# Tile 1's load behind tile 0's, three short warm matmuls, and one matmul moved earlier, in the head of a fused attention and MLP kernel

## Chip, cores, metric

One core of a Trainium2 chip. The metric is the device time of one execution in microseconds; most executions of one kernel lie within 0.3% of each other, which here is 0.4 us. "The span" is the time from the first to the last instruction of the profiled execution; it is 1.4 to 1.7 us shorter than the device time.

## The reference

Layer norm of x (2048 tokens of 448), then two branches on the normalised tokens: linear attention with 16 heads, and an MLP with a squared ReLU; the output is x plus the product of the first and the silu of the second.

```python
xn = layernorm(x)                                   # 2048 x 448, bf16
q, k, v = split(xn @ wqkv)
pq, pk = phi(q), phi(k)                             # phi(t) = t+1 if t>0 else exp(t), + 1e-6
s = ((pq @ (pk.T @ v)) / (pq @ sum(pk) + 1e-6)) @ wo    # per head
h = relu(xn @ w1 + b1) ** 2                         # 2048 x 1792
g = silu(h @ w2 + b2)
return x + s * g
```

## The kernel before

The kernel is a list of operations, put in order per engine by a planner in Python and emitted with semaphores. TensorE and the SP load queue keep the order of the program; VectorE and ScalarE are ordered by the planner's modelled times, except in the head (the first 8 us), where lists pin them.

Tokens are worked on in tiles of 128. The head normalises tiles 0 to 3, turns them with TensorE transposes (`turn`), and feeds the first products: k0 and k1 (keys of tiles 0 and 1) and h0 to h3 (the first four MLP rows). Each product has chunks of 128 of the 448 inputs. The last 64 inputs run on half of the array (64 rows). The first such matmuls, `rests(k0, k1)`, end the head: I call their start **the half-array start**.

```python
# loads, in the order of issue (SP's queue, ACT's queue)
load_x(0, 1)                                   # SP: tile 0
load_x(1, 2, "act").prio = -118                # ACT: tile 1
twins = load_k("sp", w_qkv, A_wqkv, "wk", 384, 2 * D, later=True)   # SP: 384 KB of key weights
load_x(2, 4)                                   # SP: tiles 2 and 3
dma("act", b1r[0:NF, :], ...)                  # ACT: a bias
load_w1("w1a", 0, 512, 2, [twins])             # SP: MLP weights, first part
load_x(4, 8)                                   # SP: tiles 4 to 7
load_w1("w1b", 512, 1024)
# ... (cut)
# the head's order on TensorE
warm(8, wide=True)                             # eight 512-column matmuls on ones: they wake the clock
turn("xT00", 0, (0,), "dve")                   # tile 0, chunk 0; evicted by VectorE
turn("xT01", 0, (1,), "act")
turn("xT02", 0, (2,), "act")
mains(k0, (0,), ...)
turn("xT10", 1, (0,), "act")
mains(k0, (1,), ...)
turn("xT12", 1, (1, 2), "act")
mains(k0, (2,), ...)
mains(k1, (0,), ...)
h_mains(0, (0,))                               # h0, chunk 0: 256 columns
mains(k1, (1, 2), ...)
# bias transpose (cut)
h_mains(0, (1, 2))
turn("xT03", 0, (3,), "act", 2)
h_mains(1)                                     # h1, chunks 0 to 2
turn("xT2", 2, K3, "act")
h_mains(2)
turn("xT3", 3, K3, "dve")                      # tile 3
h_mains(3)
turn("xT23", 2, (3,), "act", 2)
rests(k0, k1)                                  # the half-array start
# pinned orders: st = statistics, mv = mean/variance, ln/ex = logarithm and exponential
# for 1/sqrt, xn = normalise, xd = last 64 columns
("dve", "st0 mv0 st1 mv1 xn00 xn01 xT00 xn10 xn11 st2 mv2 st3 mv3 xn2 xd2 xn3 xd3 xT3"),
("act", "ln0 ex0 ln1 ex1 xT01 xT02 xT10 xT12 ln2 ex2 ln3 ex3 b1 xT03 xT2 xT23"),
```

Of the kernel before, what the change touches and what calls it, by code (L numbers as in the profile page):

```python
# [56 lines left out]
class Program:  # L57
# [8 lines left out]
    def add(self, eng, emit, reads=(), writes=(), dur=0.2, alts=(), nbytes=0):  # L66
        op = Op(eng, emit, reads, writes, dur, alts, nbytes)
        for t in op.reads:
            w = self.writer.get(t)
            if w is not None:  # L70
                op.raw.add(w)
            self.readers.setdefault(t, []).append(op)
        for t in op.writes:
            w = self.writer.get(t)
            if w is not None and w is not op:
                op.deps.add(w)
            for r in self.readers.get(t, ()):
                if r is not op:
                    op.deps.add(r)
            self.writer[t] = op  # L80
            self.readers[t] = [r for r in self.readers.get(t, ()) if r is op]
        op.raw.discard(op)
        op.deps |= op.raw
        for d in op.deps:
            d.succ.append(op)
        self.ops.append(op)
        return op
# [203 lines left out]
def bass_recurrent_scan__linear_attn_block__dense_activation_squared_relu__prompt_kernel(  # L291
# [4 lines left out]
    with ExitStack() as es:  # L296
# [11 lines left out]
        ones = sb("ones", [P, 2], bf)  # L308
# [95 lines left out]
        def dma(eng, dst, src, writes, nbytes, reads=()):  # L404
            return add(eng, lambda e, _: e.dma_start(dst, src), reads, writes, 0.5, nbytes=nbytes)

        def load_x(lo, hi, eng="sp", reads=()):
            names = [("x", i) for i in range(lo, hi)]
            return dma(eng, x_tok[:, lo:hi, :], x_r[:, lo:hi, :], names, (hi - lo) * P * D * 2, reads)

        def load_k(eng, w, src, name, lo, hi, eng2=None, reads=(), later=False):

            n = (hi - lo) * 2
            dma(
                eng, w[:, 0:3, lo:hi], src[0:384, lo:hi].rearrange("(c p) j -> p c j", p=P), [(name, 0)], 384 * n,
                reads,
            )
            def twins():
                for i in (0, 1):
                    dma(eng2 or eng, w[64 * i : 64 * i + 64, 3, lo:hi], src[384:448, lo:hi], [(name, 1 + i)], 64 * n)  # L420

            if later:
                return twins
            twins()
# [18 lines left out]
        table = add("act", lambda e, _: e.preload_act_table_set("natural_log_exp_and_others"), [], ["actw"], 0.1)  # L443
        table.prio = -120
        load_x(0, 1)
        load_x(1, 2, "act").prio = -118
        twins = load_k("sp", w_qkv, A_wqkv, "wk", 384, 2 * D, later=True)
        load_x(2, 4)
        dma("act", b1r[0:NF, :], B_b1.rearrange("(f p) -> f p", p=P), ["b1r"], F * 2, ["b1r"]).prio = -115
# [73 lines left out]
        def turn(name, si, chunks, eng, tiles=1):  # L523


            b = Buf("T")
            pieces = [(si + t, c) for t in range(tiles) for c in chunks]
            n = len(pieces)
            for i, (t, c) in enumerate(pieces):
                reads = xn_of(t)[min(c, 1) :][:1] or xn_of(t) if c < 3 else [("xd", t)]  # L530
                add(
                    "pe",
                    lambda e, _, i=i, t=t, c=c: e.transpose(  # L533
                        ps(b)[:, i * 64 : (i + 1) * 64].bitcast(bf), xn[:, t, c * P : (c + 1) * P], ident[:, :]
                    ),
                    reads + ["ident"] + ([b] if i else []), [b], 0.06,
                )

            def ev(e, _):
                src = ps(b)[:, 0 : n * 64].bitcast(bf)  # L540
                dst = xT[:, chunks[0], si * P : (si + tiles) * P]
                if len(chunks) > 1:
                    src = src.rearrange("p (c k) -> p c k", c=n)
                    dst = xT[:, chunks[0] : chunks[0] + n, si * P : (si + 1) * P]
                if eng == "dve":
                    return e.tensor_copy(dst, src)
                return e.activation(out=dst, in_=src, func=AF.Copy)  # L547

            dur = 0.06 + 0.09 * n if eng == "dve" else 0.16 + 0.11 * n
            head[name] = add(eng, ev, [b], [("xT", t, c) for t, c in pieces], dur)  # L550
# [51 lines left out]
        def mains(u, ks=K3, reads=None):  # L602


            def f(e, _):
                for k in ks:
                    last = u.mm(e, 2, k, k == 0, False)
                return last

            reads = u.reads if reads is None else reads  # L610
            add("pe", f, reads + ([u.bank] if ks[0] else []), [u.bank], len(ks) * MM(u.n))
# [10 lines left out]
        def phi(buf, slot, tile, shape):  # L622

            src = lambda: shape(ps(buf)[:, 0:512])
            add("act", lambda e, _: e.activation(out=slot, in_=src(), func=AF.Exp), [buf, "actw"], [tile], 0.6)  # L625
            add(
                "dve",
                lambda e, _: e.tensor_scalar(
                    out=slot, in0=slot, scalar1=1.0, scalar2=1e-6, op0=ALU.min, op1=ALU.add
                ),  # L630
                [tile], [tile], 0.25,
            )
            add(
                "dve",
                lambda e, _: e.scalar_tensor_tensor(  # L635
                    out=slot, in0=src(), scalar=1.0 + 1e-6, in1=slot, op0=ALU.add, op1=ALU.max
                ),
                [tile, buf], [tile], 0.69,
            )

        def kk(si):


            b = Buf("K")

            def mm(e, h, c, start, stop):
                return e.matmul(  # L647
                    ps(b)[:, 0:512], xT[half[h], c, si * P : (si + 1) * P], w_qkv[half[h], c, 384 : 2 * D],
                    start=start, stop=stop,
                )  # L650

            return Acc(b, xT_of(si) + wnames("wk"), mm, lambda: phi(b, qk_of(si), ("pk", si), blocks), 512)
# [419 lines left out]
        def warm(n, wide=False, after=()):  # L1072
            b = Buf("W")
            w = 512 if wide else P

            def f(e, _):
                for _i in range(n):
                    last = e.matmul(ps(b)[:, 0:w], junk[:, 0:P], junk[:, 0:w], start=True, stop=True)
                return last

            add("pe", f, ["ones", *after], [b], n * (0.426 if wide else 0.107))

        warm(8, wide=True)
        k0, k1 = kk(0), kk(1)
        first = [hh(0, fi, 0) for fi in range(4)]
        second = [hh(0, fi, 1, first[fi].bank) for fi in range(4)]

        def h_mains(fi, ks=K3):
            xs = xT_of(0) + xT_of(1)
            mains(first[fi], ks, [x for x in xs if x[2] in ks] + [("w1a", fi // 2 * 3)])  # L1090
# [2 lines left out]
        turn("xT00", 0, (0,), "dve")  # L1093
        turn("xT01", 0, (1,), "act")
        turn("xT02", 0, (2,), "act")
        mains(k0, (0,), [("xT", 0, 0)] + wk0)
        turn("xT10", 1, (0,), "act")
        mains(k0, (1,), [("xT", 0, 1)])
# [1 line left out]
        mains(k0, (2,), [("xT", 0, 2)])  # L1100
        mains(k1, (0,), [("xT", 1, 0)] + wk0)
        h_mains(0, (0,))
        mains(k1, (1, 2), [("xT", 1, 1)])
        bb = Buf("B1")
        b1v = lambda: ps(bb)[:, 0 : P // 2].bitcast(bf)
# [3 lines left out]
        )  # L1109
        h_mains(0, (1, 2))  # L1110
        turn("xT03", 0, (3,), "act", 2)
        h_mains(1)
        turn("xT2", 2, K3, "act")
        h_mains(2)
        turn("xT3", 3, K3, "dve")
# [158 lines left out]
```

## Time and profile before

| | before |
|---|---|
| device time, median of 3 | 141.1 us (140.84 to 141.34) |
| span of the profiled run | 139.4 us |
| TensorE busy | 98% |
| first transpose / half-array start | 4.17 / 8.57 us |

The profile has PE for TensorE's matmuls, PEld for its weight loads, DVE for VectorE, ACT for ScalarE. A timeline line reads: start, length, engine, source line, operation, output<-inputs, shapes, count, and in brackets the idle time just before and what ended it. A matmul's length includes its drain, so how long it occupies TensorE is read from the distance to the next start. The prediction below shows the lines of the kernel before.

### The profile page before, as it was taken

What the parts mean: (1) busy time and instruction counts of PE and PEld (TensorE: products, weight loads), DVE (VectorE), ACT (ScalarE), POOL (GpSimd) and SP (SyncE); (2) the same over time, 40 slices, a digit from 0 to 9 for tenths busy, and PEclk for the clock granted to TensorE, in tenths of its full rate; (3) what the DMA queues carried; (4) which work ended last, traced back from release to release, by engine and by line L of the source; (5) the groups of instructions that cost most, each with busy time, mean ns of one, the idle gap of its engine ahead of it and who ended that gap; (6) DMA issues with size and microseconds to landing.
All of it is one profiled execution on the core that took longest, in us unless ns stands there. A gap on an engine that the chain in (4) does not pass through costs nothing.

```text
span 139.4 us, 3131 instructions
## 1 busy us (share of the span) xinstructions
PE 136.4 (98%) x1271; PEld 69.3 (50%) x1271; DVE 92.9 (67%) x227; ACT 78.2 (56%) x153; POOL 22.9 (16%) x35
## 2 busy tenths in 40 slices
PE   9999999999999999999999999999999999999993
PEld 2484444444444444444555455645555555555472
DVE  3989798898888997789896920218936072452743
ACT  4679789788988887979887922512033030300221
POOL 2810000000000000000910000000001419092680
DMA  6996557999822300000000046970000102112132
GB/s 194 249 340 207 90 159 172 362 281 145 139 52 55 67 9 5 0 19 5 0 0 0 28 120 168 182 113 3 0 0 5 66 0 98 39 59 73 35 102 66
DMA packets 20353, 12.90 MB, mean 93 GB/s; under 512 B 9524, under 2 KB 19956, under 8 KB 20340
## 3 DMA queue, kind: packets, MB, share of 16 engines
q1 hardware_dynamic: 18332, 11.52, 33.1%
q10 hardware_dynamic: 2008, 1.19, 4.3%
q8 instruction: 10, 0.16, 0.5%
q14 instruction: 3, 0.02, 0.1%
HBM read 8.78 MB, written 2.10 MB: 78 GB/s over the span
## 4 chain that ended last, share of the span: by engine, by line
PE 95%; DMA 2%; DVE 2%; ACT 0%; issue 0%
PE pb L969 31%; PE pb L694 30%; PE pb L647 9%; PE pb L1037 8%; PE pb L728 7%; PE pb L678 6%; DMA x_tok<-in_A_x_dram 2%; PE pb L735 1%; PE pb L533 1%; DVE st L467 1%; PE pb L829 1%; PE pb L790 1%; PE pb L867 0%; DVE mv L468 0%; DVE xn L1005 0%; ACT gbuf L945 0%
## 5 line engine op out<-in xcount | busy, mean ns | idle before, releaser
L694 PE MATMUL pb<-xT,w 64*128 64x512 bf16 (+2 forms) x408 | 51.9, 365 | 0.0
L969 PE MATMUL pb<-w,r 64*128 64x448 bf16 (+3 forms) x406 | 44.9, 343 | 0.0
L703 ACT ACTIVATE r<-pb,b1f 128x512 bf16<-128x512 f32 x56 | 35.1, 688 | 3.3 <-PE pb L694 3.3
L694 PEld LDWEIGHTS pb<-xT,w 64*128 64x128 bf16 (+1 forms) x408 | 23.3, 94 | 21.0 <-DVE qk L635 0.3
L969 PEld LDWEIGHTS pb<-w,r 64*128 64x128 bf16 (+1 forms) x406 | 22.8, 95 | 20.0 <-issue 0.7
L945 ACT ACTIVATE gbuf<-gbuf 128x448 bf16<-128x448 bf16 (+1 forms) x16 | 8.7, 567 | 36.3 <-DVE gbuf L980 35.6
L980 DVE TENSOR_TENSOR gbuf<-pb,b2b 128x448 bf16<-128x448 f32 (+1 forms) x16 | 9.3, 610 | 28.3 <-PE pb L969 28.3
L1016 POOL TENSOR_TENSOR xn<-xn,x_tok 128x448 bf16<-128x448 bf16 x15 | 15.1, 1031 | 50.7 <-DVE xn L1005 50.7
L647 PE MATMUL pb<-w_qkv,xT 64*128 64x512 bf16 (+1 forms) x106 | 18.1, 378 | 0.0
L678 PE MATMUL pb<-xT,w_qkv 64*128 64x512 bf16 x84 | 15.6, 376 | 0.0
L711 DVE TENSOR_TENSOR r<-r 128x512 bf16<-128x512 bf16 x42 | 14.6, 416 | 0.9 <-ACT r L703 0.9
L394 POOL MEMSET kvm<- 128x2048 bf16 x1 | 1.8, 1804 | 58.5 <-DVE zb L672 58.5
L467 DVE BATCH_NORM_STATS2 st<-x_tok 128x6 f32<-128x448 bf16 x16 | 9.3, 612 | 2.6 <-DMA x_tok<-in_A_x_dram 2.6
L1037 PE MATMUL pb<-msb,pqT 64*128 64x448 bf16 (+3 forms) x93 | 10.9, 343 | 0.0
L635 DVE SCALAR_TENSOR_TENSOR qk<-pb,qk 128x512 bf16<-128x512 f32 x16 | 10.6, 684 | 0.2
L625 ACT ACTIVATE qk<-pb 128x512 bf16<-128x512 f32 x16 | 8.9, 595 | 3.0 <-PE pb L647 2.5
L1005 DVE TENSOR_TENSOR xn<-pb,gbuf 128x448 bf16<-128x448 f32 (+2 forms) x17 | 9.2, 591 | 1.8 <-ACT gbuf L945 1.1
L647 PEld LDWEIGHTS pb<-w_qkv,xT 64*128 64x128 bf16 (+1 forms) x106 | 6.8, 94 | 6.2 <-ACT xT L547 0.5
L728 PE MATMUL pb<-qk,xn 128*128 128x448 bf16 x48 | 9.3, 353 | 0.0
L678 PEld LDWEIGHTS pb<-xT,w_qkv 64*128 64x128 bf16 x84 | 6.1, 94 | 4.8
L712 ACT ACTIVATE r<-r 128x512 bf16<-128x512 bf16 x14 | 8.4, 638 | 0.0
L666 DVE TENSOR_TENSOR zacc<-zacc,qk 128x448 f32<-128x448 f32 x13 | 8.1, 623 | 0.3
(74 smaller groups left out, 97.3 us busy)
## 6 DMA issues: line engine op xcount, KB each, us to landing
out_dram<-xn SPq DMA_DIRECT2D x15, 112.0 KB, 1.7
w<-in_B_w_dram SPq DMA_DIRECT2D x1, 1568.0 KB, 10.0
x_tok<-in_A_x_dram SPq DMA_DIRECT2D x3, 448.0 KB, 3.8
xT<-rows ACTq DMA_DIRECT2D x6, 112.0 KB
w<-in_B_w_dram SPq DMA_DIRECT2D x1, 576.0 KB, 5.7
xT<-rows SPq DMA_DIRECT2D x5, 112.0 KB
w_o<-in_A_wo_dram SPq DMA_DIRECT2D x1, 392.0 KB, 11.1
w_qkv<-in_A_wqkv_dram SPq DMA_DIRECT2D x1, 384.0 KB, 3.7
```

The source lines that it names most:

```text
L467: add("dve", lambda e, _: e.bn_stats(st6[:, si, :], x_tok[:, si, :]), [("x", si)], [("st", si)], 0.58),
L635: lambda e, _: e.scalar_tensor_tensor(out=slot, in0=src(), scalar=1.0 + 1e-6, in1=slot, op0=ALU.add, op1=ALU.max),
L647: return e.matmul(ps(b)[:, 0:512], xT[half[h], c, si * P : (si + 1) * P], w_qkv[half[h], c, 384 : 2 * D], start=start, stop=stop,)
L678: return e.matmul(ps(b)[:, 0:512], w_qkv[half[h], c, m * P : (m + 1) * P], xT[half[h], c, g * 512 : (g + 1) * 512], start=start, stop=stop,)
L694: return e.matmul(ps(b)[:, c0 : c0 + n], w_1[half[h], c, fi * P : (fi + 1) * P], xT[half[h], c, t : t + n], start=start, stop=stop,)
L703: lambda e, _: e.activation(out=slot, in_=ps(b)[:, 0:512], func=AF.Relu, bias=b1f[:, fi : fi + 1]),
L711: return e.tensor_tensor(out=slot, in0=slot, in1=slot, op=ALU.mult)
L728: last = e.matmul(ps(b)[:, 0:D], xn[:, si, c * P : (c + 1) * P], pk_of(si), start=(si == 0), stop=(si == NT - 1),)
L969: return e.matmul(ps(b)[:, 0:n], r2[half[h], fi, si * P : (si + 1) * P], w_2[half[h], fi, c], start=start, stop=stop)
L980: "dve", lambda e, _: e.tensor_tensor(out=gs, in0=ps(b)[:, 0:n], in1=b2b[:, c], op=ALU.add),
L1016: eng, lambda e, _: e.tensor_tensor(out=ob, in0=ob, in1=x_tok[:, si, c], op=ALU.add),
L1037: return e.matmul(ps(b)[:, 0:n], q, m, start=start, stop=stop)
```

## The change

The intent, as read from the edit: tile 0's load should not share the DMA engines with tile 1's; the clock should not fall asleep in the hole between the warm matmuls and the first transposes; and a hole of 0.1 us before k1's second chunk should be filled.

```diff
-        load_x(1, 2, "act").prio = -118
+        load_x(1, 2, "act", ["ones"]).prio = -118
...
         warm(8, wide=True)
+        warm(2)
...
         turn("xT02", 0, (2,), "act")
+        warm(1)
         mains(k0, (0,), [("xT", 0, 0)] + wk0)
...
         h_mains(0, (0,))
+        h_mains(1, (0,))
         mains(k1, (1, 2), [("xT", 1, 1)])
...
         turn("xT03", 0, (3,), "act", 2)
-        h_mains(1)
+        h_mains(1, (1, 2))
         turn("xT2", 2, K3, "act")
```

## The prediction

> **What bounds the kernel now.** I read the page first. The TensorE (PE) row is busy for 136.4 of 139.4 us and the chain that ended last is PE for 95%, so time can be won only where PE stands idle or runs slowly. The change touches only the first 8 us, so I then read the timeline of PE there, the chain in order of time, and the timelines of VectorE (DVE), ScalarE (ACT) and the DMA queues around each hole.
>
> ```profile
> span 139.4 us, 3131 instructions
> PE 136.4 (98%) x1271; PEld 69.3 (50%) x1271; DVE 92.9 (67%) x227; ACT 78.2 (56%) x153; POOL 22.9 (16%) x35
> PE 95%; DMA 2%; DVE 2%; ACT 0%; issue 0%
> ...
> 0.30 3.60 PE L1078 MATMUL pb<-ones 128*128 128x512 bf16 x8 [0.30 <-DVE ones L358]
> 4.17 0.71 PE L533 MATMUL pb<-ident,xn 128*128 128x128 bf16 x3 [0.27 <-DVE xn L490]
> 4.77 0.58 PE L647 MATMUL pb<-w_qkv,xT 128*128 128x512 bf16 x1
> 5.17 0.24 PE L533 MATMUL pb<-ident,xn 128*128 128x128 bf16 x1
> 5.25 0.38 PE L647 MATMUL pb<-w_qkv,xT 128*128 128x512 bf16 x1
> 5.46 0.28 PE L533 MATMUL pb<-ident,xn 128*128 128x128 bf16 x2
> 5.57 0.59 PE L647 MATMUL pb<-w_qkv,xT 128*128 128x512 bf16 x2
> 6.00 0.27 PE L694 MATMUL pb<-xT,w 128*128 128x256 bf16 x1
> 6.21 0.60 PE L647 MATMUL pb<-w_qkv,xT 128*128 128x512 bf16 x2
> ```
>
> A matmul's duration includes its drain; the time it takes from the next one is the distance between starts. The eight warm matmuls lie 0.427 us apart (3.60 less one drained 0.63, over 7 is 0.424), so the last one starts at 3.27 and stops feeding at 3.70. Then: idle to 4.17; three transposes held to the pace of DVE (starts 4.17, 4.48, 4.56); the first matmul of k0 at 4.77, which takes 0.40 before the next start, where those at 5.57 take 0.22 each; and a hole between h0's first chunk (6.00, 0.11 us of feeding) and 6.21. From there I found starts back to back until 8.42, a change of row mode of 0.10 at 8.57, then nothing open until 74 us.
>
> What sets 4.17 is the chain from tile 0's load: landing, then four DVE instructions in order (tile 1's statistics stand before tile 0's normalisation):
>
> ```profile
> 0.00 2.32 DMA x_tok<-in_A_x_dram
> 2.34 0.63 DVE L467 BATCH_NORM_STATS2 st<-x_tok 128x6 f32<-128x448 bf16 x1 [2.14 <-DMA x_tok<-in_A_x_dram]
> 3.00 0.18 DVE L468 BATCH_NORM_AGGREGATE mv<-st 128x2 f32<-128x6 f32 x1
> 3.10 0.59 DVE L467 BATCH_NORM_STATS2 st<-x_tok 128x6 f32<-128x448 bf16 x1
> 3.73 0.18 DVE L468 BATCH_NORM_AGGREGATE mv<-st 128x2 f32<-128x6 f32 x1
> 3.83 0.60 DVE L490 TENSOR_SCALAR xn<-x_tok,mv,rstd 128x128 bf16<-128x128 bf16 x2
> ```
>
> The last thing to read is what the head feeds into. PE's only early wait after it is a weight load at 11.36:
>
> ```profile
> 8.89 1.15 DVE L467 BATCH_NORM_STATS2 st<-x_tok 128x6 f32<-128x448 bf16 x2 [0.30 <-DMA x_tok<-in_A_x_dram]
> 10.43 0.30 ACT L477 ACTIVATE vep<-mv,eps 128x2 f32<-128x2 f32 x1 [0.34 <-DVE mv L468]
> 10.63 0.67 ACT L703 ACTIVATE r<-pb,b1f 128x512 bf16<-128x512 f32 x1
> 10.54 1.03 PE L647 MATMUL pb<-w_qkv,xT 64*128 64x512 bf16 x8
> 11.36 0.36 PEld L694 LDWEIGHTS pb<-xT,w 64*128 64x128 bf16 x6 [0.29 <-DVE qk L635]
> 11.40 0.60 PE L694 MATMUL pb<-xT,w 64*128 64x512 bf16 x4
> ```
>
> The load is put down to DVE, but DVE's first eviction (10.48 plus 0.68) was done at 11.16, 0.2 before; ACT's eviction of h0 ends at 10.63 + 0.67 = 11.30, and 0.06 is what such a release takes elsewhere (DVE ends 4.11, PE starts 4.17). So I take ACT as the releaser. ACT came late because it stood 0.34 for the statistics of tiles 4 and 5, and those stood 0.30 for their load, issued at 4.96 and landing 3.9 later on a busy DMA (shares of 9 in most slices from 5 to 9). Nothing in that chain depends on PE's head. PE arrives at 11.40 with 0.04 us to spare.
>
> **What the Trainium skill says.** "TensorE: Matmul & The Clock Gate", Part 1, has PE start at half clock and go to full after a busy window of about 3.4 us that runs free of the kernel; 512 columns then take 426.7 ns cold and 215.7 warm. The trace agrees: 0.427 before, 0.22 from 5.25 on. The 0.40 at 4.77 is nearly all cold, so in this execution the step came at about 5.15 (0.375 cold and 0.026 warm make up 512 columns). The profile's granted clock reads 1.000 throughout and does not show this step. Part 4 of the same page says transposes do not count as busy in the same way; no view here shows it. "DMA: Bandwidth & Descriptors", Issuing engines are not separate DMA queues, says loads issued from SP and ACT run on the same 16 engines and interleave: the trace has tile 1's packets (second queue) beside tile 0's from 1.3 us on.
>
> **The change part by part.**
>
> Tile 1's load. ACT now issues it at 0.15; it will wait for the ones, set at 0.14 + 0.06 = 0.20. PE waits for the same and starts at 0.30, so the issue moves by about 0.15 to 0.30. It takes 2.4 us to land: 2.70 in place of 2.55 (more exactly 2.59). DVE wants it at 3.10, so 0.4 is left: no loss. The gain is what tile 0 stops losing to it. The DMA view in slices of 0.1 us gives 16 packets for the first queue at 1.2 with the second silent, and 17 at 1.6 beside 15 of the second: tile 0 is not slowed while its 128 packets go out (1.0 to 1.8). Only the last 0.5 us to landing can shorten. I take 0.05, at most the 0.15 of the shift.
>
> Two warm matmuls behind the eight: 2 x 0.107 (a quarter of 0.427 each) in the hole from 3.70 to 4.17: end 3.91, off the path. Cost 0.
>
> One warm matmul before k0: the third transpose starts at 4.56 and feeds 0.107 cold, to 4.67; k0 starts at 4.77, released by the DVE copy (4.49 + 0.22 = 4.71). The hole is 0.10, the matmul 0.107: cost 0.01.
>
> h1's first chunk behind h0's: 256 columns, 0.107 to 0.11 us, same weight piece and same inputs as h0's chunk at 6.00, so no new wait. It fills the hole from 6.11 to 6.21, which ends by ACT's eviction (5.45 + 0.71 = 6.16). It is taken from its place after 7.04, so PE saves 0.11 there less 0.01 of delay: 0.10.
>
> Clock. If the step stays at 5.15, work moved 0.05 earlier runs at half speed: -0.02. In the executions where added activity brings it forward to before 4.77, k0's first matmul gives 0.19 more.
>
> Sum at 8.57: 0.05 - 0.01 + 0.10 - 0.02 = 0.12 us earlier. But at 11.36 PE meets the ACT chain, which is tied to the load of tiles 4 to 7. Only the 0.04 of slack gets through; the other 0.08 turns into idle before 11.40. With 0.04 off 141.1 it is 141.06.
>
> **The rivals.**
>
> The planner reorders. The kernel orders ACT and DVE by modelled times, and these move a little with the warm matmuls and h1. If ACT evicts h0 before the logarithm of tiles 4 and 5, the gate falls and all 0.12 arrives: about 141.0. For: h0's product is nearly complete when ACT stands idle for 0.34. Against: the first orders are pinned, and the modelled load does not move. I give it 35%.
>
> The warm matmuls work through the clock. Then the head gains 0.2 to 0.3 more, and the time is 140.8 where the gate is open. For: the hole from 3.70 to 4.17 lies in the window. Against: even without them the window up to 5.15 was enough to raise the clock, and 0.32 us of work is under a tenth of 3.4. 15%.
>
> The gate lies elsewhere in most executions: the three runs span 0.5 us, so the clock's phase and DMA times differ. Where the head is later than in the profile (141.34), the change gains its full 0.12 or more.
>
> Loss: tile 1 late, a bad eviction order or a clock step that fails. The 0.4 of slack and the unchanged order of loads speak against it; it would make 141.3 to 141.6. 10%.
>
> **Range and chances.** Weighted: half at 0.04, a third at 0.12, the rest between 0.3 and -0.3, gives about 0.1 to 0.15. I say 140.95. The runs of one kernel spread by 0.25 to either side, and a median of three halves that, plus the 0.3 a moved clock or order is worth: 140.5 to 141.3. For 2% it would need 2.8 us; all holes of the head together (0.47, 0.20, 0.10, 0.18 cold, 0.10) make about 1.05. So within 2%: 0.98.
>
> **What would show it right or wrong.** Right: ACT's queue issues tile 1 at about 0.30, it lands near 2.7; tile 0's first statistics start within 2.20 to 2.34; two chunks of 256 columns stand between 5.9 and 6.2 with no hole; the row-mode change comes 0.1 to 0.15 earlier than 8.57; and the 512-column H matmuls still start at about 11.35 behind a PE hole of near 0.1. Wrong: PE passes 11.4 with no hole and early (planner), the first k0 matmul taking 0.22 (clock), or statistics of tile 1 waiting for a DMA.

## The result, and the profile after

The changed kernel takes 141.00 us (median of 6, 140.84 to 141.27) against 140.97 for the one before (6 runs). The ratio is 1.0002, 95% interval 0.9984 to 1.002: the same. The interval is wider than the gain that was predicted, so the times alone can neither show nor exclude a gain of 0.1 us. A ratio here is the mean time of one kernel's fast runs over that of the other's of the same rounds, so not quite the ratio of the medians quoted.

From the page of the changed kernel:

```profile
span 139.3 us, 3137 instructions
PE 136.3 (98%) x1274; PEld 68.5 (49%) x1274; DVE 93.0 (67%) x227; ACT 78.2 (56%) x153; POOL 22.9 (16%) x35
```

From its timeline of PE:

```profile
0.30 3.52 PE L1078 MATMUL pb<-ones 128*128 128x512 bf16 x10 [0.30 <-DVE ones L358]
...
4.10 0.60 PE L533 MATMUL pb<-ident,xn 128*128 128x128 bf16 x3 [0.28 <-DVE xn L490]
4.53 0.22 PE L1078 MATMUL pb<-ones 128*128 128x128 bf16 x1
4.65 0.39 PE L647 MATMUL pb<-w_qkv,xT 128*128 128x512 bf16 x1
...
5.97 0.39 PE L694 MATMUL pb<-xT,w 128*128 128x256 bf16 x2
6.20 0.59 PE L647 MATMUL pb<-w_qkv,xT 128*128 128x512 bf16 x2
...
7.79 0.34 PE L533 MATMUL pb<-ident,xn 128*128 128x128 bf16 x3
...
8.51 0.39 PE L647 MATMUL pb<-w_qkv,xT 64*128 64x512 bf16 x2
```

Compare line by line. The first transpose starts at 4.10 in place of 4.17. k0's first matmul starts at 4.65 in place of 4.77 and already runs at full clock: in this execution the clock stepped up at 3.39, during the eighth wide warm matmul, before any of the added ones ran. So PE had gained 0.23 us by k1's first chunk (5.56 in place of 5.79, the second start of the x2 lines). Then most of it is gone: h0's and h1's chunks start at 5.97 (h0's was at 6.00), k1's second at 6.20 (6.21), now with h1's chunk already done. At the first chunk of h2 PE is 0.14 ahead (7.40 in place of 7.54), about what the prediction had summed up; it then stands idle 0.06 before tile 3's transposes. At 8.51 the head is 0.06 ahead, and it stays so to the end: the last matmul starts at 136.74 in place of 136.81.

Two waits took the gain. The first is in the view of waits of PE's weight loads between 5 and 9 us; the second shows on DVE's timeline, where tile 3's normalisation ends at 7.32 + 0.41 = 7.73, and the transposes of it start 0.06 later (above, 7.79):

```profile
PEld pb L694 <- DMA w<-in_B_w_dram: 0.4, 1, 0.4
...
5.15 0.63 DVE L467 BATCH_NORM_STATS2 st<-x_tok 128x6 f32<-128x448 bf16 x1
...
7.32 0.41 DVE L490 TENSOR_SCALAR xn<-x_tok,mv,rstd 128x384 bf16<-128x384 bf16 x1
```

The kernel before has the same wait in reach; its lines of DVE and PE are

```profile
7.33 0.41 DVE L490 TENSOR_SCALAR xn<-x_tok,mv,rstd 128x384 bf16<-128x384 bf16 x1
...
7.87 0.33 PE L533 MATMUL pb<-ident,xn 128*128 128x128 bf16 x3
```

There TensorE came to tile 3 last, without idling; but VectorE had it ready only 0.07 earlier (7.33 + 0.41 + 0.06 = 7.80).

The first wait is not one of h1's chunk. It is that of h0's chunk for the first MLP weights, which landed at 5.92; the kernel with the short warm matmuls alone, without h1's chunk, has it too (landed 6.06, start 6.10).

The statistics of tile 2 at 5.15 follow the landing of tiles 2 and 3, which the trace puts at 5.13. In the kernel before these statistics started at 5.17, after VectorE's own work. From tile 2's statistics to tile 3's transposes it is a fixed chain (2.61 to 2.64 us in the seven executions where TensorE waits for it).

The gate that the prediction named is there, but open. PEld's line of it:

```profile
11.22 0.22 PEld L694 LDWEIGHTS pb<-xT,w 64*128 64x128 bf16 x4 [0.21 <-DVE qk L635]
```

The weight load came at 11.22 for a matmul at 11.34, and PE did not idle there. In this execution tiles 4 to 7 landed at 8.72 and not at 8.87, and ScalarE's eviction ended at 11.15 in place of 11.30.

### The profile page after: what moved, and what is told of

It is laid out like the page before. It is cut to its first block, busy times and chain, and to the rows that moved or that the text cites. A ratio compares the mean times of both kernels' runs of the same rounds, so it can differ in the third digit from the quotient of the medians.

```text
span 139.3 us, 3137 instructions
## 1 busy us (share of the span) xinstructions
PE 136.3 (98%) x1274; PEld 68.5 (49%) x1274; DVE 93.0 (67%) x227; ACT 78.2 (56%) x153; POOL 22.9 (16%) x35
## 4 chain that ended last, share of the span: by engine, by line
PE 95%; DVE 2%; DMA 2%; ACT 0%; issue 0%
PE pb L969 31%; PE pb L694 31%; PE pb L647 9%; PE pb L1037 8%; PE pb L728 7%; PE pb L678 7%; DMA x_tok<-in_A_x_dram 2%; PE pb L735 1%; DVE st L467 1%; PE pb L829 1%; PE pb L533 1%; PE pb L790 1%; PE pb L867 0%; DVE xn L490 0%; DVE mv L468 0%; DVE xn L1005 0%
## 5 line engine op out<-in xcount | busy, mean ns | idle before, releaser
L694 PEld LDWEIGHTS pb<-xT,w 64*128 64x128 bf16 (+1 forms) x408 | 22.7, 94 | 22.1 <-DMA w<-in_B_w_dram 0.4
```

The costliest lines, as they stand in the source:

```text
L694: return e.matmul(ps(b)[:, c0 : c0 + n], w_1[half[h], c, fi * P : (fi + 1) * P], xT[half[h], c, t : t + n], start=start, stop=stop,)
```

## The experiments

Twelve kernels, each with a profile, so twelve more executions to read. The theories, as they were formed: **A**, VectorE paces the head; **B**, TensorE paces it and the parts add as in the prediction; **C**, three things decide together (the clock's step, VectorE's chain, the load of tiles 4 to 7); **D**, the form of C with numbers that the first ten traces gave. All results were correct.

### The load alone (e1_load)

Edit: only `load_x(1, 2, "act", ["ones"])`.

> Only tile 1's load behind the ones. Theory A (up to 7.8 us the head is paced by VectorE, which works without a break from tile 0's landing to the last normalisation): tile 0's statistics start near 2.27 in place of 2.34, the first transpose near 4.10, tile 3's transposes at 7.79 or a little later, the first half-array matmul at 8.50 to 8.57. Theory B (TensorE paces the head, and the parts add as in the prediction): first half-array matmul 0.05 to 0.07 before 8.57. Both: time within 0.2% of before, not to be told from 1.

140.99 us against 140.98, ratio 0.9998 (0.9981 to 1.0014). Tile 0's statistics started at 2.33, tile 3's transposes at 7.75, the half-array start was 8.46. The last two lie 0.04 before A's figures, and the half-array start as much before B's. What fits A is the wait: VectorE has tile 3 ready at 7.69, and TensorE had idled 0.05. But tile 0 landed at 2.31, no earlier than before (2.32), so a gain by the load does not show here.

### The short warm matmuls alone (e2_warm)

Edit: only `warm(2)` and `warm(1)`.

> Only the three short warm matmuls. Both theories: in holes, so no cost and no gain, first half-array matmul at 8.57 within 0.05, time ratio 1.000 within 0.002. If the warm matmuls work through the clock (rival), the first 512-column matmul of k0 takes 0.22 here and 0.40 in a run without them; if the step of the clock is a matter of phase, it falls anywhere between 3 and 6 us whether the three are there or not.

141.06 us, ratio 1.0003 (0.998 to 1.0026). Half-array start 8.63, 0.01 outside the range expected, set by tiles 2 and 3, which landed at 5.29. k0's first matmul took 0.24 to the next start, at full clock; the step came at 3.69, as the wide ones ended. By the expectation that would speak for the rival, but the kernels with the load alone and with h1's chunk alone, without the short matmuls, also have 0.24 there.

### h1's chunk alone (e3_h1)

Edit: only the two `h_mains(1, ...)` lines.

> Only h1's first chunk behind h0's. Theory B: the hole of 0.10 before 6.21 is filled and the first half-array matmul comes 0.10 earlier, at 8.47. Theory A: tile 3's transposes cannot start before VectorE has normalised tile 3 (7.74 plus 0.06), so at most 0.07 of it arrives, half-array matmul not before 8.50, with a new hole before tile 3's transposes.

141.16 us, ratio 1.0013 (0.9996 to 1.003). As A has it: the hole at 6.1 is gone, and a hole of 0.16 stands before tile 3's transposes (7.82, half-array start 8.53). And here the gate at 11.4 shut. Tiles 4 to 7 landed at 9.10 in this execution; the timelines of DVE, ACT and PEld:

```profile
9.13 1.15 DVE L467 BATCH_NORM_STATS2 st<-x_tok 128x6 f32<-128x448 bf16 x2 [0.57 <-DMA x_tok<-in_A_x_dram]
...
10.66 0.29 ACT L477 ACTIVATE vep<-mv,eps 128x2 f32<-128x2 f32 x1 [0.61 <-DVE mv L468]
10.86 0.67 ACT L703 ACTIVATE r<-pb,b1f 128x512 bf16<-128x512 f32 x1
...
11.60 0.36 PEld L694 LDWEIGHTS pb<-xT,w 64*128 64x128 bf16 x6 [0.57 <-DVE qk L635]
```

Each is 0.23 to 0.24 later than its line in the prediction. ACT's eviction ends at 11.53 and the weight load follows 0.07 later; the releaser that the profile names is DVE, but DVE's first eviction was done at 10.72 + 0.68 = 11.40. PE stood 0.27 there, and the time of this execution is 141.41.

### Tile 3's normalisation first (e4_order)

Edit, on the changed kernel: `xn2 xd2 xn3 xd3` becomes `xn2 xn3 xd2 xd3` in VectorE's list.

> The changed kernel with tile 3's main normalisation moved ahead of tile 2's last columns on VectorE (0.3 us earlier for tile 3's transposes). Theory A: the pin at 7.79 goes, tile 3's transposes start at 7.55 to 7.65 and the half-array matmuls at 8.30 to 8.40 in place of 8.50; the wait of TensorE at 11.2 to 11.4 on the eviction behind the load of tiles 4 to 7 then stands in the way with a hole of 0.05 to 0.2, so time changes by at most 0.1 us. Theory B: nothing changes before 8.50.

141.4 us, ratio 1.0021 (1.0003 to 1.0039). A miss, by a fault of mine. Tile 3 cannot be normalised before ScalarE has its scale, so VectorE only moved its idle time forward (timelines of DVE and ACT):

```profile
7.55 0.38 DVE L490 TENSOR_SCALAR xn<-x_tok,mv,rstd 128x384 bf16<-128x384 bf16 x1 [0.23 <-ACT rstd L481]
...
7.31 0.20 ACT L481 ACTIVATE rstd<-vep 128x1 f32<-128x1 f32 x1
```

So the "VectorE chain" runs through ScalarE at its end. In this execution the clock stepped only at 6.2; TensorE itself set tile 3's transposes at 8.22, and the experiment does not test A. Why the six runs together come out 0.2% slower is open: only one of them has a trace.

### Two loads for tiles 4 to 7 (e5_split)

Edit, on the changed kernel: `load_x(4, 8)` becomes `load_x(4, 6); load_x(6, 8)`. All compute engines keep their order.

> The changed kernel with the load of tiles 4 to 7 issued as two loads (4 and 5, then 6 and 7); all compute engines keep their order. Theory C (three things that TensorE's head does not move decide together when the dense work passes 11.4 us: the step of the clock, the VectorE chain to tile 3, and the load of tiles 4 to 7 behind ScalarE's logarithm): tiles 4 and 5 land 0.3 or more earlier, VectorE's statistics of tile 4 follow at 8.6 without a DMA wait, and the weight load that waited to 11.2 or 11.6 is there before 11.1, without a hole; time lower by 0 to 0.2 us. Risk: the next weight loads are issued 0.6 later and hold up the same place. Theory B (TensorE alone paces): no change in time or at 11.4.

141.34 us, ratio 1.0019 (0.9995 to 1.0043); the six runs fall in two groups, 140.87 to 141.03 and 141.65 to 141.76. The statistics of tile 4 started without a DMA wait (8.24), and ACT's eviction ended 0.3 early, at 10.84. But the risk came true: the weights behind this load landed later (the last piece of the first group at 11.25, against 10.48 in the changed kernel), PE stood 0.31 at 11.45, and again later, in PE's timeline:

```profile
17.50 0.37 PE L694 MATMUL pb<-xT,w 64*128 64x512 bf16 x1 [0.69 <-DMA w<-in_B_w_dram]
```

Relief at one gate was paid back at the next loads. For the hole at 11.45 the profile names VectorE's eviction (ended 11.34) and not the weights (landed 11.25, with the weight load at 11.42); which of the two it was is not settled. That the later issue alone made the weights late is not shown either.

### ScalarE's exchange (e6_swap, e7_before_swap)

Edit: after planning, h0's eviction is put ahead of the logarithm of tiles 4 and 5 on ScalarE; once on the changed kernel, once on the kernel before.

```diff
         pr.schedule()
+        act = pr.order["act"]
+        i = next(j for j, o in enumerate(act) if ("vep", 4) in o.writes)
+        ln45, r0 = act[i], act[i + 1]
+        act[i], act[i + 1] = r0, ln45
+        ln45.start, r0.start = r0.start, ln45.start
         pr.emit(nc, es)
```

> The changed kernel with two ScalarE instructions exchanged by hand: h0's eviction ahead of the logarithm of tiles 4 and 5. Theory C: ScalarE's eviction starts at 10.1 in place of 10.5, ends 0.4 earlier, and the wait at 11.2 to 11.4 is no longer set by the load of tiles 4 to 7 through ScalarE; it can still be set through VectorE's eviction, which leaves some 0.15 more slack. Where the head comes early the gain arrives: time lower by 0 to 0.15 us. Theory B: no change.

> The kernel before with the same exchange. If the gate at 11.4 were the only thing that hides the change, the difference between this one and the one with the change and the exchange is the predicted 0.12 us (0.09%) or more; if the clock step and the VectorE chain also hide it, the two agree within 0.1%.

With the change 140.9 us, ratio 0.9997 (0.9978 to 1.0016); without it 140.89, ratio 0.9987 (0.997 to 1.0004). They differ by 0.1% with intervals that overlap widely, and not in the direction of the change. The exchange did what it should (timelines of ACT and PEld of the changed kernel with it):

```profile
10.23 0.69 ACT L703 ACTIVATE r<-pb,b1f 128x512 bf16<-128x512 f32 x1 [0.34 <-PE pb L694]
10.82 0.28 ACT L477 ACTIVATE vep<-mv,eps 128x2 f32<-128x2 f32 x1
...
11.12 0.41 PEld L694 LDWEIGHTS pb<-xT,w 64*128 64x128 bf16 x6 [0.24 <-DVE qk L635]
```

ACT is done at 10.92, and the weight load comes at 11.12 for a matmul at 11.22. So opening the gate uncovers no gain of the change. That agrees with other waits hiding it as well, but does not prove it: each interval spans 0.5 us, and the gain looked for is 0.12.

### No warm matmuls (e8_cold)

Edit, on the changed kernel: both `warm` lines ahead of the transposes and the one before k0 removed.

> The changed kernel with no warm matmuls at all. The clock step then comes [...]at 7.5 to 11 us, instead of 3.4 to 6.2; the head's matmuls take twice as long until then. First half-array matmul at 10 to 11.5 in place of 8.5, time up by 1.2 to 2.5 us (ratio 1.008 to 1.018). If the head did not depend on the clock, the time would stay.

142.85 us, ratio 1.0125 (1.0107 to 1.0143), as expected: the clock stepped at about 9.1, the half-array start was 10.33. The clock does matter; the eight wide matmuls settle it, the three short ones added nothing that shows.

### Tile 0 in halves (e9_halves, e10_halves_x23)

Edit, on the kernel before with h1's chunk and the exchange: tile 0 loaded as rows 0 to 63 by SP and rows 64 to 127 by ACT; in the second one also `load_x(2, 4, "act")`. Tile 0's statistics wait for both halves.

```diff
-        load_x(0, 1)
+        dma("sp", x_tok[0:64, 0, :], x_r[0:64, 0, :], [("x", 0)], ...)
+        dma("act", x_tok[64:P, 0, :], x_r[64:P, 0, :], [("x", 0, "b")], ...).prio = -119
         load_x(1, 2, "act").prio = -118
```

> The kernel before with h1's chunk, with the ScalarE exchange, without short warm matmuls, and with tile 0 loaded as two halves of 64 rows over both queues at once. Theory D, from the ten traces so far: tile 3's transposes start at the latest of three times: tile 0's landing plus 5.44 us, the landing of tiles 2 and 3 plus 2.65, and what TensorE's clock step allows; the half-array matmuls 0.71 later; the end follows those at a fixed distance. So tile 0 lands at 1.8 to 2.0 in place of 2.0 to 2.4, the first transpose near 3.7, and tile 3's transposes at 7.35 to 7.95, mostly set by tiles 2 and 3 (landing 4.7 to 5.3) instead of tile 0; time lower by 0 to 0.3 us. Theory B (the holes of TensorE are what counts): filling h1's hole alone gives 0.1 and the landing gives nothing more.

> The same with the load of tiles 2 and 3 issued by ScalarE behind tile 1's, beside the first weights. Theory D: tiles 2 and 3 land at 3.5 to 4.4, so that tile 0's chain sets tile 3's transposes again: 7.3 to 7.5 (tile 0's landing plus 5.44), the half-array matmuls at 8.0 to 8.2, time lower by 0.2 to 0.4 us (ratio 0.997 to 0.9985) where the clock step comes before 5 us. Risk: the first weights land later (4.4 or more) and hold k0, so that TensorE sets tile 3's transposes near 7.6.

143.82 us, ratio 1.0221 (1.019 to 1.0253), and 144.01 us, ratio 1.019 (1.0151 to 1.0228; five of its six runs are fast, one is slow). Both expectations failed, on two counts. Tile 0's second half landed at 2.38, no earlier than the whole tile. And tile 1, issued second on ACT's queue, was issued at 0.77, 0.14 after the key weights (0.63), and landed at 4.68: 3.9 us after issue, against 2.3 in the changed kernel, where it is issued ahead of them. In the second kernel it was the same (0.77 to 4.76), the first weights landed at 4.54, and tiles 2 and 3, expected at 3.5 to 4.4, landed at 6.04. DVE's and PE's timelines, and the row of the granted clock in 40 slices (3.6 us each), of the first one:

```profile
4.70 0.63 DVE L467 BATCH_NORM_STATS2 st<-x_tok 128x6 f32<-128x448 bf16 x1 [1.45 <-DMA x_tok<-in_A_x_dram]
...
5.80 0.54 PE L533 MATMUL pb<-ident,xn 128*128 128x128 bf16 x3 [2.06 <-DVE xn L490]
...
PEclk9959999999999999999999999999999999999999
```

PE idled 2.06 us; the clock then fell back to half from 6.9 to 10.3 us (512-column matmuls 0.43 apart; the 5 in the third slice), so that the head ended at 11.55. In the second kernel the matmuls ran at half clock up to about 8.9, and the head ended at 11.13. What these two show is how close the changed line may stand to a cliff: delaying tile 1's issue from 0.15 to 0.23 cost nothing that shows; in these two, where it was issued after the key weights, the time was about 3 us longer (2.7 to 3.1 by the ratios). Whether that comes of the place behind the key weights, of the second place in ACT's queue or of the halves was not tested apart.

### TensorE delayed, VectorE delayed (e11_pe_delay, e12_dve_delay)

Edits, on the changed kernel: `warm(1)` before k0 becomes `warm(5)`; and a useless memset on VectorE before tile 0's normalisation.

```diff
+        head["pad"] = add("dve", lambda e, _: e.memset(lnd[:, :], 0.0), [], ["lnd"], 0.4)
...
-            ("dve", "st0 mv0 st1 mv1 xn00 ...
+            ("dve", "st0 mv0 st1 mv1 pad xn00 ...
```

> The changed kernel with five short warm matmuls ahead of k0 in place of one, so TensorE's own work in the head grows by 0.22 us (full clock) to 0.43 us (half clock). Theory D (tile 3's transposes wait for VectorE's chain, tile 0's landing plus 5.44, or tiles 2 and 3 plus 2.65, whenever the clock has stepped early): in such an execution tile 3's transposes move by at most 0.1 and the time by at most 0.1 us; where the clock steps late they move by 0.3 to 0.45. Theory B (TensorE paces): the end moves by the full 0.22 to 0.43 in every execution, ratio 1.0016 to 1.003.

> The changed kernel with one useless VectorE memset (128 x 512) between tile 1's statistics and tile 0's normalisation; its length is read from the trace (I expect 0.3 to 0.55 us). Theory D: tile 3's transposes come that much later than tile 0's landing plus 5.44, the half-array matmuls and the end with them: time up by the memset's length less up to 0.1, ratio 1.002 to 1.004. Theory B: TensorE has 0.26 us of holes before the first transpose and between them, so the end moves by less than half of it.

The first: 141.0 us against 141.28 for the kernel before of the same rounds, ratio 0.9986 (0.9968 to 1.0004). Lines from its timelines of PE and DVE:

```profile
4.57 0.45 PE L1078 MATMUL pb<-ones 128*128 128x128 bf16 x5
4.86 0.38 PE L647 MATMUL pb<-w_qkv,xT 128*128 128x512 bf16 x1
...
7.26 0.41 DVE L490 TENSOR_SCALAR xn<-x_tok,mv,rstd 128x384 bf16<-128x384 bf16 x1
...
7.72 0.34 PE L533 MATMUL pb<-ident,xn 128*128 128x128 bf16 x3
```

The five short matmuls pushed k0 back to 4.86, 0.29 after the first of them. Yet tile 3's transposes start at 7.72, 0.05 after VectorE has the tile (7.26 + 0.41 = 7.67), and TensorE had stood 0.08 idle before them. The half-array start is 8.44, earlier than in the changed kernel. So this execution swallowed 0.2 us more work on TensorE ahead of the gate. That speaks against B, under which it would have had to arrive; so do the times, whose interval ends at 1.0004 where B had 1.0016 or more.

The second: 141.29 us against the same 141.28, ratio 1.0002 (0.9986 to 1.0018). Two lines of its DVE timeline:

```profile
3.89 0.48 DVE L1063 MEMSET lnd<- 128x512 f32 x1
...
7.62 0.37 DVE L490 TENSOR_SCALAR xn<-x_tok,mv,rstd 128x384 bf16<-128x384 bf16 x1
```

The next instruction started 0.40 after the memset, at 4.29. At the end of VectorE's chain 0.37 of that is left (7.99 + 0.06 = 8.05, where 7.68 follows from tile 0's landing without the memset). But the clock stepped at about 5.9 in this execution, and TensorE itself came to tile 3's transposes only at 8.24, so its trace does not test D cleanly. In time, the six runs (mean 141.33) are 0.26 above the six of the first kernel (mean 141.08) on the same chip: the direction of D, two thirds of the size. Against the kernel before nothing shows; on this chip that kernel itself ran 0.3 above its medians of the other calls (140.92 to 140.98). The two kernels compared also differ in the short matmuls (1 and 5). The second experiment supports D only in part.

### All traces together

Times in us from the span's start. "Rule" is the later of tile 0's landing + 5.44 and the landing of tiles 2 and 3 + 2.65: the two ways through VectorE and ScalarE to tile 3's transposes. Both constants were fitted to the first ten traces that landed in order, so only the last two rows test them. T3 is the start of tile 3's transposes, "half" the half-array start; the last column is the device time less "half". "TensorE" marks the rows where it came to tile 3 last, without idling; "by" means that TensorE stood idle while the clock stepped. The two kernels with tile 0 in halves are left out, since tile 1 landed late there.

| kernel | time | tile 0 landed | tiles 2, 3 landed | clock step | rule | T3 | half | time - half |
|---|---|---|---|---|---|---|---|---|
| before | 141.06 | 2.32 | 4.95 | 5.15 | 7.76 | 7.87, TensorE | 8.57 | 132.49 |
| changed | 140.99 | 2.25 | 5.13 | 3.39 | 7.78 | 7.79 | 8.51 | 132.48 |
| load alone | 140.88 | 2.31 | 4.76 | by 4.47 | 7.75 | 7.75 | 8.46 | 132.42 |
| warm alone | 141.04 | 2.30 | 5.29 | 3.69 | 7.94 | 7.92 | 8.63 | 132.41 |
| h1 alone | 141.41 | 2.38 | 4.90 | by 4.55 | 7.82 | 7.82 | 8.53 | 132.88, holes |
| tile 3 first | 141.40 | 2.23 | 5.36 | 6.2 | 8.01 | 8.22, TensorE | 8.92 | 132.48 |
| two loads | 141.76 | 2.14 | 4.69 | 3.3 | 7.58 | 7.59 | 8.30 | 133.46, holes |
| exchange, changed | 140.86 | 2.14 | 4.92 | 5.2 | 7.58 | 7.68, TensorE | 8.38 | 132.48 |
| exchange, before | 140.61 | 2.02 | 4.70 | 3.0 | 7.46 | 7.46 | 8.17 | 132.44 |
| no warm | 142.80 | 2.18 | 4.45 | 9.1 | 7.62 | 9.63, TensorE | 10.33 | 132.47 |
| TensorE delayed | 140.86 | 2.29 | 4.59 | 3.8 to 4.45 | 7.73 | 7.72 | 8.44 | 132.42 |
| VectorE delayed | 141.46 | 2.24 | 5.03 | 5.9 | 8.05 with memset | 8.24, TensorE | 8.95 | 132.51 |

Three things are to be seen. "Half" follows T3 by 0.70 to 0.72 in every row, and the time follows "half" by 132.4 to 132.5 in every row but the two with holes further on. T3 is the rule's value within 0.02 where TensorE is early, and later where the clock stepped at 5.15 or after: there TensorE sets it. And no effect of the three short warm matmuls on the step is to be seen: with them (changed, warm alone, tile 3 first, two loads, exchange on the changed kernel, TensorE delayed, VectorE delayed) it lies between 3.3 and 6.2, without them (before, load alone, h1 alone, exchange on the kernel before) between 3.0 and 5.15, all behind the same eight wide ones. With seven executions against four and such a scatter, a shift of some tenths would not show.

Tile 0 landed at 2.14 to 2.31 in the eight executions with the moved load (mean 2.22) and at 2.02 to 2.38 in the four without it (mean 2.25). A gain of 0.03 within a spread of 0.36 is no finding.

What stays open: on one chip the times of the kernel before lie in two groups, 140.83 to 140.92 and 141.22 to 141.30, on the others less clearly. The step's phase and the landings move "half" by as much in the table, but without a profile of each timed run this is argued, not shown. Effects of the parts under 0.2% could not be told apart by the times; what is said of them rests on single traces. No version was shown to beat both kernels: the exchange on the kernel before is lowest (140.89), its interval reaches 1.0004, and its trace had the earliest landing of tile 0 of all.

## Why the prediction was right or wrong

The time (140.95 against 141.00 measured) and "within 2%" were right. But the closeness of the number is luck. The prediction took 0.15 off 141.1, the median of three runs; six runs of the kernel before gave 140.97, so that no gain was measured, and one kernel's runs span 0.5 us. Its weighting does not come out either: half at 0.04 and a third at 0.12 make 0.06, not 0.1 to 0.15, which would have been 141.04. By its steps:

- **The load.** Moved later as told, but by 0.08 (issued at 0.23), where 0.15 had been taken. It landed at 2.56, ahead of VectorE's wish at 3.03: no loss, as predicted. The predicted gain of 0.05 was not found: the landing of tile 0 scatters by several times that.
- **The warm matmuls in the holes.** Cost 0 and about 0.01: right. In the changed kernel k0 starts at 4.65, 0.05 after VectorE's copy ends (4.37 + 0.23), so the matmul before it held nothing up.
- **The clock.** The prediction held the step for a matter of phase and gave 15% to the rival in which the short matmuls bring it forward. In the changed kernel's trace the step did come early, and PE did gain 0.23. Taken alone, that trace would have been read as the rival come true; but the step came before the first added matmul, and over the traces it comes early and late with and without them.
- **h1's chunk, "so no new wait".** That held: h1's chunk followed h0's by 0.12. What the working did not ask is when h0's own inputs were ready. In the kernel before, the weights had landed at 5.77, ahead of TensorE at 6.00; with TensorE early, h0's chunk waited for them (landed at 5.92, start 5.97), and most of the early clock step was lost there. The kernel with h1's chunk alone shows the hole at 6.1 filled as worked out (starts 5.91, 6.02, 6.13). In the changed kernel's trace there was no such hole to fill: ScalarE's eviction ended at 5.93, before h0's chunk started.
- **"Sum at 8.57: 0.12".** The parts were added on TensorE alone; measured were 0.06, after 0.14 just before tile 3's transposes. The step left out is the gate between: VectorE's and ScalarE's chain to tile 3's transposes. In the profile of before it ended at 7.33 + 0.41 + 0.06 = 7.80 with TensorE arriving at 7.87, so 0.07 was all that TensorE could gain ahead of it. I had found "starts back to back until 8.42" and not asked how much earlier each input was ready. The kernel with TensorE delayed shows the same gate from the other side.
- **The gate at 11.4.** That ScalarE's eviction and not VectorE's is the releaser was right: it shut in the trace of h1 alone, and with the exchange that eviction ended 0.2 ahead of the weight load. But in the changed kernel's own trace it was open, since tiles 4 to 7 landed at 8.72 and not at 8.87, and all 0.06 got through. So the 0.04 that the prediction let through was nearly met in this one trace, by another gate than the one named; that too is luck, since landings alone move the head by more.
- **The planner's rival.** It did not come about: VectorE and ScalarE keep their orders in the changed kernel.
- **Its own signs.** Tile 0's first statistics (2.27) and the two chunks without a hole (5.97 to 6.20) came as listed. The row-mode change came 0.06 earlier and not 0.1 to 0.15, and no hole stood before the H matmuls at 11.34. Two of its signs of being wrong came, or nearly: k0's first matmul took 0.24 (0.22 listed), and PE passed 11.4 early without a hole. But the first goes with a clock step before any added matmul, and the second with an earlier landing of tiles 4 to 7 and not with another order of the planner.

The theories: A (VectorE paces) describes the executions with an early step, B (TensorE paces, the parts add) fails in the kernel with TensorE delayed, and D, which takes the later of the two, fits the traces; of the two traces made to test it, one bears out its VectorE side and the other does so only in part.

## What to carry to other kernels

A hole in the busiest engine is worth only the slack of the next point where that engine waits for another: before adding up what a change saves, read for each consumer downstream when its inputs were ready, not only whether it waited. Where a start-up chain hangs on landings and on a clock step that scatter by several tenths of a microsecond, one profile before and one after can show a cause that is chance; look at several executions, with and without the change. A load that may slip a little without harm may still not slip behind the next one queued: in the two kernels where it did, the time was about 3 us longer, against a hoped-for 0.05, though they changed other loads too.

## What the Trainium skill lacked or had wrong

- "DMA: Bandwidth & Descriptors", Issuing engines are not separate DMA queues, says that loads from different engines run on the same 16 engines and interleave. The kernel with tile 0 in halves shows less interleaving than that suggests: tile 1's load, issued by ACT 0.14 us after SP's 384 KB, landed 3.9 us after issue, against 2.3 when issued ahead of it. ACT's queue moved 0 to 4 packets per 0.2 us from 2.0 to 3.4 us, then 57 in the slice at 3.6. The section does not say that a load issued a little later on another engine can be held back so long; why it was is not shown.
- "TensorE: Matmul & The Clock Gate", Part 4, says that full clock does not engage for transposes. Here they run at the clock of the matmuls around them: 0.107 us from one to the next before the step, 0.056 after it (the exchange on the changed kernel, step at about 5.2).
- The same page, Part 1, has the step vary with the phase of a free-running window; it gives half a microsecond to either side in one place, though in another it tells of a kernel with 6, 11 or 14 cold matmuls. Here the wider spread is the fitting one: the step fell between 3.0 and 6.2 us with the same eight wide matmuls from 0.30 us on. For the fall it has at least one idle window of about 3.4 us; in the kernel with tile 0 in halves 2.06 us of idleness and then 1.1 us with six matmuls stood before the fall at 6.9 us.
- Part 1 also warns that the trace's events of the clock gate can be unreliable, but no page that I read says that the profile's granted clock does not show the first step: it reads 9 or more in the first slice, while the wide matmuls are 0.427 apart, yet it does show the fall in the third slice of the kernel with halves.
- No page that I read gives the scatter of landings between executions: here 2.02 to 2.38 us for tile 0 and 8.51 to 9.10 us for tiles 4 to 7.
